# A state-space block and a feed-forward block in one kernel: token groups cut across batches

## The chip, the cores and the metric

The kernel runs on one core of a Trainium2 chip. The metric is the device time of one execution in microseconds, as the median of several runs. A core has a matrix engine (TensorE, in the profile PE, with its weight loads as PEld), a vector engine (VectorE, DVE), a scalar engine (ScalarE, ACT), a general engine (GpSimd, POOL) and a sync engine (SyncE, SP) that here only issues DMAs. Each engine works through its own list of instructions in order; between engines semaphores order the work. ACT and SP issue DMAs from their own lists, so an issue that has to wait holds up what stands behind it in that list.

## The reference

Two blocks follow each other. The first is a Mamba-2 scan with 4 batches, 8 heads, 768 tokens, head size 32, state size 16:

```python
chunk = 32
log_a = np.log(np.clip(a, 1e-06, 1.0))
for c in range(nc):
    cum = np.cumsum(la, axis=-1)
    L = np.exp(cum[:, :, :, None] - cum[:, :, None, :]) * causal
    M = np.einsum('bhin,bhjn->bhij', Cc, Bc) * L
    y_intra = np.einsum('bhij,bhjd->bhid', M, xc)
    y_inter = np.einsum('bhin,bhnd->bhid', Cc, state) * np.exp(cum)[..., None]
    y[:, :, sl] = y_intra + y_inter
    Bx = np.einsum('bhjn,bhjd->bhjnd', Bc, xc) * np.exp(cum[:, :, -1:] - cum)[..., None, None]
    state = np.exp(np.sum(la, axis=-1))[..., None, None] * state + np.sum(Bx, axis=2)
```

Its output, laid out as 3072 tokens (batch times sequence) by 256, goes through a feed-forward block with float64 weights of 256 x 2048 and 2048 x 256:

```python
h = x @ w_in
g = h * (1.0 / (1.0 + np.exp(-1.702 * h)))
return (g @ w_out).astype(np.float32)
```

All inputs but the weights are float32, and so is the output. The result does not depend on the chunk length; the kernel takes chunks of 64 tokens.

## The kernel before

**Tiling.** Tokens are worked in NG = 6 groups of TG = 512. A group has two pairs (PG = 2), a pair has two 128-token chunks, a 128-token chunk has two sides of 64 tokens, `SIDES`. Pair p stands for 128-token chunks 2p and 2p + 1 of the tokens counted through the batches: batch b and chunk c come from `divmod(2 * p, NC)` with NC = 6. So group 0 is the first 512 tokens of batch 0, group 1 its last 256 and the first 256 of batch 1, and so on. States run through the 64-token steps of one batch one after the other.

**The scan of one pair.** Decay matrices L come, for group 0, from cumulated logarithms (`cum`, by ACT's Ln and a DVE scan, then the matmuls of `differ`, line 554, and ACT's Exp, `decay_exp`, line 575); for pair 2 from a fan-out on PE and scans (`fan_all`); for later pairs from one DVE scan over the spread of a (`decay`, line 402). The spread is a DMA that copies a row of a scratch tensor to 64 partitions (`spread`, line 256). `ends` and `ends_first` make B times the decay to the chunk's end (Be), `score` the products C B^T (cb, line 680), `weigh` multiplies L by them (line 691), `gain` forms what a chunk adds to the state (A, line 711). `keep_first` (group 0) and `keep_both` (later groups) add gains up to states S; in group 0 by a DVE scan over all eight steps, with `drops` and `parts_first` preparing its operands. `finish` sums `intra` (line 828) and `inter` (line 816: C from the start of the chunk, CsT, times the state before) and ACT copies the sum to yT.

**Rows of decay since a chunk's start.** `since` is what `inter` and the states need. `spread_rows` loads a whole batch's row of a to all partitions (line 265), `clip_rows` and `decay_rows` turn it into `since[b]`; for batch 0 it comes from matmuls (`since_first`, and `fan_since` with `since_fanned`, lines 501 and 530).

**B and C.** For groups 0 and 2 to 5 they are loaded as blocks (zB, zC; `load_first` line 134, `load_blocks` line 124) and turned by DVE transposes (`turn_first` line 615, `turn_blocks` line 635); `turn_back` makes B by tokens again on PE for group 0.

**The feed-forward weights.** They arrive as float64 in ten pieces (`fetch`, line 180) and are narrowed to float32 on DVE and ACT: `fields` (lines 192, 195), `clamp` (ACT, lines 203, 204), `rounded` (line 208) and `join` (lines 222, 228). `fetch(1, held=True)` starts with a DVE memset of the tile, which is what lets its DMA go. `spread` has the same argument.

**The feed-forward block.** Groups 0 and the start of 1 are plain matmuls (`hidden` line 884, `project_all` line 982). From then on 2 x 2 block products are made with 7 multiplications: `first` (lines 940, 950; the copies by ACT are line 945, the SiLU line 917, the sums by DVE line 1072) and `product` (lines 1045, 1052), with operands mixed on DVE (`mix_in`, `mix_y`, `mix_g`, `mix_w`). In `first`, one PSUM bank X takes step "1", is copied by ACT, then takes step "6" on top, is copied, then "7" and "4": each of these matmuls waits for the copy before it. `turn_out` transposes a finished group on DVE and stores it by four DMAs per half (line 1103).

**What sets the order.** The order of each engine is written by hand: lists `in_hidden`, `in_project` and `after` hang work on places of group 0 and 1, and strings such as "4.1 4.5 4.2 P P 4.6 P L P 4.7 P P P 4.D" are run step by step (L is `more_loads`, which begins with the spread of pair 6). At the end `in_order` binds each engine to that order.

**Queues.** The build hands eight DMA semaphores out in turn to the DMAs of SP and ACT.

## Time and profile before

| what | us |
|---|---|
| median of 3 runs (350.42 to 353.03) | 351.38 |
| span of the profiled execution | 348.2 |
| PE busy in it | 341.8 |
| DVE, ACT, POOL busy | 254.8, 151.4, 14.0 |
| PE busy in 0 to 5, 5 to 10, 10 to 15, 15 to 20, 20 to 25 us | 3.79, 3.94, 4.76, 4.67, 4.43 |
| PE busy in 30 to 70 us | 40.0 |
| DVE busy in 50 to 60, 60 to 70, 70 to 80, 80 to 90 us | 9.35, 9.07, 9.86, 8.43 |
| first matmul of the hidden layer starts (line 884) | 17.47 |
| the second run of them, after the second weight piece, starts | 21.74 |
| DMA: packets, MB, share of 16 engines | 89980, 25.92, 34.1% (SP's and ACT's large queue) |

A line of a timeline gives the start in us from the beginning of the span, the length in us, the engine (a q behind it: its sequencer, which issues DMAs), the line of the kernel, the operation, what is written and read, the shape, and how often; in brackets stand the idle time of the engine before it and what ended that. The chain of waits is followed back from the last instruction, at each step to what released it. Times of one execution are compared with its own span; 3.2 us of the median lie outside it.

### The profile page before, as it was taken

The numbers are of one execution on the slowest core, as the hardware profiler recorded it, in microseconds if no ns is written. First come the engines' busy times: TensorE is split into PE (matmuls) and PEld (weight loads), VectorE is DVE, ScalarE is ACT, GpSimd is POOL, SyncE is SP. The second block draws the span as 40 slices with busy tenths as digits, with TensorE's granted clock in tenths as the row PEclk, the third lists the DMA queues.
The fourth block names the chain that finished last, engine by engine and source line by source line (L and its number), as shares of the span: only waits on it lengthen the run. The fifth ranks groups of instructions, "written<-read, shape, count | busy, mean of one in ns | idle before, by whom it ended". The sixth has DMA issues, their size and how long they took to land.

```text
span 348.2 us, 8126 instructions
## 1 busy us (share of the span) xinstructions
PE 341.8 (98%) x3386; PEld 273.1 (78%) x3386; DVE 254.8 (73%) x476; ACT 151.4 (43%) x348; POOL 14.0 (4%) x42
## 2 busy tenths in 40 slices
PE   7899999999999999999999999999999999999996
PEld 6634444557888888888888888888888888899996
DVE  5999999998679998839996548788454654455463
ACT  5598583107354323744342544432554321554320
POOL 8400000100000100000000000000000000000000
PEclk9999999999999999999999999999999999999999
DMA  6599997444527100445703027300000300000301
GB/s 158 118 347 200 260 219 172 78 85 80 107 53 133 44 0 10 69 93 102 111 22 55 2 75 121 65 0 3 0 4 2 61 2 0 0 2 0 62 0 61
DMA packets 89980, 25.92 MB, mean 74 GB/s; under 512 B 73432, under 2 KB 87128, under 8 KB 89944
## 3 DMA queue, kind: packets, MB, share of 16 engines
q1 hardware_dynamic: 89112, 24.88, 34.1%
q10 hardware_dynamic: 832, 0.52, 0.5%
q8 instruction: 26, 0.43, 0.5%
q14 instruction: 10, 0.08, 0.1%
HBM read 22.15 MB, written 3.24 MB: 73 GB/s over the span
## 4 chain that ended last, share of the span: by engine, by line
PE 93%; DMA 3%; DVE 3%; issue 1%; SPq 0%; DVEq 0%
PE acc L1045 28%; PE X L940 19%; PE Y L950 14%; PE h L884 9%; PE o L982 8%; PE acc L1052 7%; PE y L828 2%; PE cb L680 2%; PE y L816 1%; DMA bits<-in_moe_w_in_dram 1%; PE A L711 1%; DMA zB<-in_B_dram 1%; DMA az<-in_a_dram 1%; DVE p L192 1%; DVE m L208 0%
## 5 line engine op out<-in xcount | busy, mean ns | idle before, releaser
L945 ACT ACTIVATE ac<-X 128x256 f32<-128x256 f32 x76 | 29.0, 382 | 78.6 <-PE X L940 78.2
L1045 PE MATMUL acc<-mg,mw 128*128 128x256 f32 x192 | 54.5, 379 | 0.0
L917 ACT ACTIVATE gT<-gT 128x512 f32<-128x512 f32 (+1 forms) x76 | 39.3, 520 | 34.2 <-DVE gT L1072 33.5
L1072 DVE TENSOR_TENSOR gT<-Y,ac 128x512 f32<-128x512 f32 x38 | 26.2, 688 | 36.5 <-PE Y L950 29.9
L940 PE MATMUL X<-my,mi 128*128 128x256 f32 x152 | 45.2, 380 | 0.0
L1072 DVE TENSOR_TENSOR gT<-Y,b 128x256 f32<-128x256 f32 x38 | 15.8, 419 | 34.5 <-PE Y L950 34.5
L1045 PEld LDWEIGHTS acc<-mg,mw 128*128 128x128 f32 x192 | 36.5, 190 | 5.0
L884 PE MATMUL h<-yT,w_in 128*128 128x512 f32 (+2 forms) x108 | 35.7, 486 | 0.6 <-DVE w_in L228 0.6
L1045 PE MATMUL acc<-gT,w_out 128*128 128x256 f32 x128 | 35.5, 379 | 0.0
L884 PEld LDWEIGHTS h<-yT,w_in 128*128 128x128 f32 x108 | 18.3, 190 | 16.4 <-issue 13.2
L940 PEld LDWEIGHTS X<-my,mi 128*128 128x128 f32 x152 | 28.0, 190 | 4.1 <-ACT ac L945 0.4
L982 PE MATMUL o<-gT,w_out 128*128 128x512 f32 x64 | 28.6, 597 | 0.0
L908 DVE TENSOR_TENSOR mg<-gT 128x512 f32<-128x512 f32 x40 | 27.2, 681 | 0.0
L1045 PEld LDWEIGHTS acc<-gT,w_out 128*128 128x128 f32 x128 | 24.2, 190 | 3.4 <-ACT yT L855 0.2
L945 ACT ACTIVATE b<-X 128x256 f32<-128x256 f32 x38 | 14.6, 383 | 20.0 <-PE X L940 19.6
L940 PE MATMUL X<-yT,w_in 128*128 128x256 f32 x76 | 23.2, 389 | 0.0
L950 PE MATMUL Y<-yT,w_in 128*128 128x256 f32 x76 | 22.7, 381 | 0.0
L950 PE MATMUL Y<-my,mi 128*128 128x256 f32 x76 | 22.6, 379 | 0.0
L940 PE MATMUL X<-my,w_in 128*128 128x256 f32 x76 | 22.6, 381 | 0.0
L950 PE MATMUL Y<-yT,mi 128*128 128x256 f32 x76 | 22.5, 379 | 0.0
L982 PEld LDWEIGHTS o<-gT,w_out 128*128 128x128 f32 x64 | 11.8, 190 | 13.2 <-issue 12.4
L402 DVE TENSOR_TENSOR_SCAN L<-a,idents 128x1024 f32<-128x1024 f32 x9 | 20.5, 2278 | 0.4 <-DMA a<-scratch 0.4
(154 smaller groups left out, 544.5 us busy)
## 6 DMA issues: line engine op xcount, KB each, us to landing
a<-scratch SPq DMA_DIRECT2D x18, 256.0 KB, 5.2
bits<-in_moe_w_out_dram SPq DMA_DIRECT2D x8, 512.0 KB, 5.7
x<-in_x_dram SPq DMA_DIRECT2D x24, 128.0 KB, 3.3
out_dram<-ob SPq DMA_DIRECT2D x40, 64.0 KB, 1.9
bits<-in_moe_w_in_dram SPq DMA_DIRECT2D x8, 256.0 KB, 4.5
bits<-in_moe_w_in_dram SPq DMA_DIRECT2D x4, 512.0 KB, 9.2
b<-in_B_dram SPq DMA_DIRECT2D x20, 64.0 KB, 3.0
af<-in_a_dram SPq DMA_DIRECT2D x3, 384.0 KB
```

The source lines that it names most:

```text
L402: nc.vector.tensor_tensor_scan(out=L, data0=ra[p].rearrange("p k e -> p (k e)"), data1=idents.rearrange("p h i -> p (h i)"), initial=0.0, ...
L680: nc.tensor.matmul(out=s["cb"][side, r, k].rearrange("p (q i) -> p q i", q=Q), lhsT=BT[rows, k, side], rhs=CT[rows, k, :, side], start=Tru ...
L884: nc.tensor.matmul(out=h[:, cols], lhsT=w_in[:, f, k], rhs=yT[g][:, k, cols], start=(k == 0 and e == 0), stop=(k == NK - 1), skip_group_ch ...
L908: nc.vector.tensor_tensor(out=t[:, 0:2], in0=B[:, :, 1], in1=B[:, 0], op=ALU.subtract)
L917: nc.scalar.activation(o, i, AF.Silu, scale=GELU_SCALE)
L940: nc.tensor.matmul(out=s["X"], lhsT=lhsT, rhs=rhs, start=i == "1", stop=i == "4", skip_group_check=True)
L945: nc.scalar.activation(copy, s["X"], AF.Copy)
L950: nc.tensor.matmul(out=o, lhsT=lhsT, rhs=rhs, start=s.pop("new", False), stop=i != "5", skip_group_check=True)
L982: nc.tensor.matmul(out=o[c], lhsT=w_out[:, c, f], rhs=gT[g, f // 2][:, f % 2], start=(f == 0), stop=(f == NF - 1), skip_group_check=True)
L1045: nc.tensor.matmul(out=acc[g][0][i][:, cols], lhsT=w, rhs=h[:, cols], start=(j == 0 and k == 0 and (i, 0) in begins), stop=(j == NF // 2 - ...
L1052: nc.tensor.matmul(out=o[k] if type(o) is list else o[:, cols], lhsT=h[:, cols], rhs=w, start=(j == 0 and (i, k) in begins), stop=(j == NF ...
L1072: nc.vector.tensor_tensor(out=o, in0=v, in1=w, op=ALU.add)
```

## The change

A group is now one 128-token chunk of each of the four batches: pair p stands for chunk p // 2 of batches 0 and 1 (p even) or 2 and 3 (p odd), by `place`. So all four batches' states go forward together, two steps per group. Group 0's decays are cumulated over 128 columns for all 32 rows (batch and head) and not over 256 for 16; `differ` issues twice as many matmuls of half the width. The state of group 0 comes from ACT's copies of the gains and one multiply and add (`keep_first`, `carry_first`) in the place of the scan over eight steps. The second half of group 0's gains is formed after `finish`. Later states are made by `keep`: a product with the decay, then one DVE instruction per head of a quarter that takes the gains from PSUM. Rows of a are loaded per group, four DMAs for each; block loads of C and B take both of a group's pairs at once, eight DMAs each; a half group's store is 16 DMAs. The first loads have a new order and new queues, and x of pair 0 is issued by ACT between its Ln and its Exp table load. `fetch(1)` and the following ones come before `score`, `fields(0)` and `rounded(0)` later. `dense` gives way to `unread`, which puts three wide matmuls with unused results around the first `intra`.

```diff
-    def load_first(name, queues):
+    def place(p):
+        c, n = divmod(p, PG)
+        return c, 2 * n
+
+    def load_blocks(g, name, queues):
         src = {"B": B, "C": C}[name]
...
+            for q in range(Q):
+                queues[(Q * r + q) % len(queues)].dma_start(
+                    out=t[32 * r:32 * r + 32, q],
+                    in_=src[:, Q * r + q, g * P:(g + 1) * P].rearrange("b (i f) n -> i b (f n)", i=32))
...
-    def spread_rows(b):
-        raf[b] = raw.tile([P, NC, P], FP32, tag="af", name=f"af{b}", bufs=1)
-        nc.sync.dma_start(out=raf[b].rearrange("p c s -> p (c s)"),
-                          in_=a[b].unsqueeze(1).to_broadcast([NH, N, S]))
+    def spread_rows(g):
+        raf[g] = raw.tile([P, NB, P], FP32, tag="af", name=f"af{g}", bufs=2)
+        for b in range(NB):
+            nc.sync.dma_start(out=raf[g][:, b], in_=a[b, :, g * P:(g + 1) * P].unsqueeze(1).to_broadcast(
+                [NH, N, P]))
...
-    for r in range(R):
-        (nc.sync, nc.scalar)[r % 2].dma_start(
-            out=az0[32 * r:32 * r + 32].rearrange("p k s -> p (k s)"),
-            in_=a[:2, :, :TG].rearrange("b h (c s) -> (b h) c s", c=PG))
+    nc.sync.dma_start(out=az0, in_=a.rearrange("b h s -> (b h) s")[:, :P].unsqueeze(0).to_broadcast(
+        [R, NB * NH, P]))
...
-    load_first("C", [nc.scalar] * R)
-    load_first("B", [nc.sync] * R)
+    load_blocks(0, "C", [nc.scalar, nc.sync])
+    load_blocks(0, "B", [nc.scalar, nc.sync, nc.sync, nc.scalar, nc.sync, nc.sync, nc.scalar, nc.sync])
     fetch(0)
-    load(0, "x")
     load(1, "x")
...
     nc.scalar.activation(cum, az0, AF.Ln)
+    load(0, "x", nc.scalar)
     table(AF.Exp)
...
+    def keep_first(i):
+        if i == 0:
+            state[0] = ssd.tile([P, 2, NB, Q * D], FP32, tag="S", name="S0")
+        a, new = by_head(increment.pop((0, i))), by_head(state[0][:, i])
+        for q in range(Q):
+            nc.scalar.activation(new[:, :, q], a[:, :, q], AF.Copy, scale=part[:, q:q + 1])
+
+    def decayed(g, i):
+        t = ssd.tile([P, NB, Q * D], FP32, tag="old", name=f"old{g}_{i}", bufs=1)
+        e = i * H + H - 1
+        nc.vector.tensor_tensor(out=t, in0=state[g][:, 0] if i else state[g - 1][:, 1],
+                                in1=since[g][:, :, e:e + 1].to_broadcast([P, NB, Q * D]),
+                                op=ALU.mult)
+        return t
+
+    def carry_first():
+        plus(state[0][:, 1], state[0][:, 1], decayed(0, 1))
...
         for r in range(R):
             cols = slice(i * P + 32 * r, i * P + 32 * r + 32)
-            nc.sync.dma_start(out=rows[:, :, cols],
-                              in_=t[32 * r:32 * r + 32].rearrange("p (b e) -> p b e", e=32))
+            for b in range(NB):
+                nc.sync.dma_start(
+                    out=rows[:, b, :, cols],
+                    in_=t[32 * r:32 * r + 32, b * P:(b + 1) * P].rearrange("p (u e) -> p u e", e=32))
...
-    fields(0)
     ends_first(0)
     ends_first(1)
-    rounded(0)
-    score(range(PG), since_first)
-    weigh(0)
     fetch(1, held=True)
     for i in range(2, 6):
         fetch(i)
     rows_a(az, (nc.sync,))
+    score(range(PG))
+    since_first()
+    fields(0)
+    weigh(0)
     weigh(1)
-    drops()
-    gain(range(PG))
-    parts_first()
     for p in range(PG):
         since_start(p, nc.gpsimd)
+    gain(range(PG), (0,))
+    keep_first(0)
     clamp(0)
-    keep_first()
-    dense(2)
     finish(range(PG))
-    dense(0)
+    gain(range(PG), (1,))
+    keep_first(1)
+    rounded(0)
     join(0)
     fields(1)
     clamp(1)
+    carry_first()
```

## The prediction

> **What bounds the kernel now.** I read the page first, then the chain of waits in order of time, then the timelines of each engine over the first 22 us and over 76 to 113 us.

> ```profile
> span 348.2 us, 8126 instructions
> PE 341.8 (98%) x3386; PEld 273.1 (78%) x3386; DVE 254.8 (73%) x476; ACT 151.4 (43%) x348; POOL 14.0 (4%) x42
> PEclk9999999999999999999999999999999999999999
> PE 93%; DMA 3%; DVE 3%; issue 1%; SPq 0%; DVEq 0%
> ```

> TensorE (PE) is busy all through. In the chain it is the last to end from 21.74 us, where the second weight piece has been converted, until the closing stores. So a change can move the time in three ways: when PE begins its unbroken stretch, how much PE work lies in it, and whether a wait reaches PE inside it. First the start, ScalarE's timeline (start, length, engine and line, what, idle time before it):

> ```profile
> 3.75 0.44 ACTq L134 DMA_DIRECT2D zC<-in_C_dram  x1
> 4.81 0.42 ACT L343 ACTIVATE cum<-az 128x256 f32<-128x256 f32 x1 [1.17 <-DVE az L341]
> 5.25 1.28 ACT L285 ACT_TABLE_LOAD   x1
> 7.43 1.02 ACT L575 ACTIVATE L<-ab 128x1024 f32<-128x1024 f32 x1 [0.68 <-PE ab L554]
> 8.66 1.21 ACT L575 ACTIVATE L<-ab 128x256 f32<-128x256 f32 x4 [0.20 <-PE ab L554]
> ```

> Here the exponentials wait for PE, 0.68 and 0.20 us. Then a later place, SyncE's DMA queue (SPq), VectorE (DVE) and ACT:

> ```profile
> 78.25 1.00 SPq L150 DMA_DIRECT2D x<-in_x_dram  x2
> 88.01 0.67 SPq L265 DMA_DIRECT2D af<-in_a_dram  x1
> 91.40 5.40 SPq L1103 DMA_DIRECT2D out_dram<-ob  x8
> 101.87 1.27 SPq L256 DMA_DIRECT2D a<-scratch  x2
> ...
> 107.68 2.29 DVE L402 TENSOR_TENSOR_SCAN L<-a,idents 128x1024 f32<-128x1024 f32 x1 [0.42 <-DMA a<-scratch]
> 110.42 0.42 DVE L1072 TENSOR_TENSOR gT<-Y,b 128x256 f32<-128x256 f32 x1
> ...
> 110.87 0.42 ACT L917 ACTIVATE gT<-gT 128x256 f32<-128x256 f32 x1 [2.13 <-DVE gT L1072]
> 111.19 0.37 ACT L945 ACTIVATE ac<-X 128x256 f32<-128x256 f32 x1
> ...
> 112.03 0.59 PE L940 MATMUL X<-my,mi 128*128 128x256 f32 x2
> ```

> This is one chain. SP issues the spread of a for pair 6 at 101.87; its landing is the one DMA that any L402 scan waits for (0.42). Behind that scan in DVE's order stands the sum at 110.42; ACT sits 2.13 us for it; behind that on ACT stands the copy at 111.19, which ends at 111.56; the matmul at 112.03 adds to the same bank and may not start before. PE's slack there is 112.03 - 111.56 = 0.47 us. SP itself was idle from 88.68 to 91.40 and from 96.80 to 101.87, 2.72 + 5.07 = 7.8 us.

> **The start, step by step.** The build hands out eight DMA semaphores in turn over SP and ACT together: a DMA may be issued once the eighth before it has landed. That is in the order of the built programs, and the rows show it (the last zC is issued at 3.75 although ACT's issue before ended at 3.70). Rows: an issue takes 0.42 to 0.44 us (the first on each queue 0.6 to 0.8), landing is 2.0 to 2.7 us after issue; I take 2.3. Before, 12 loads come ahead of the weights (4 az, 4 C, 4 B); after, 17 (1, 8, 8).

> SP after: az at 0.80, C at 1.6, 2.25, 2.7, 3.2, B at 3.7, 4.5, 5.0, 5.5, 6.0 (from the second B on held by the C eight before). ACT: C at 0.95, 1.5, 2.0, then 3.8 (waits for the C of 1.6), B at 4.3, 4.8, 5.25. ACT's Ln stands behind that last issue, so it starts at 5.7 and not 4.81, although az, now one DMA, lands earlier. Behind Ln stand pair 0's two x issues, each waiting for a B load that SP issued: 5.0 + 2.3 = 7.3 and 5.5 + 2.3 = 7.8. Behind them stands the Exp table load: 7.8 + 0.55 + 1.28 + 0.2 = 9.9 us for the first exponential, 2.5 us later than 7.43. PE no longer limits it (its masks' sums end near 9.6: half the scan width saves some 0.3 of 0.69 us, twice the small L554 matmuls cost some 0.2 per pair by the 0.86 us that 64 records of A take). The five exponentials then run back to back and end at 9.9 + 1.02 + 1.21 = 12.1, against 9.87.

> Part of it is given back. Be started 0.6 us late (10.48) because DVE was at `fields(0)`, whose first step took 1.72 us beside POOL's L648 and 0.43 us elsewhere. After: Be to 12.8, fields 0.85, weigh 2.35, so weigh ends at 16.0 against 14.09. Removed behind it: the scan over states 1.22 and its two copies 0.70 on DVE, the POOL copy 0.99. Added there: a multiply and an add of 128x256 (`carry_first`, 2 x 0.42), which wait for ACT's copies of the second half's gains. Of the 28 inter matmuls 16 remain, 0.95 of 1.67 us; 16 of the 32 gains now stand between them and h, 0.4. So h begins near 18.6 (17.47 before). The second piece: first piece ready at 16.0 + 3 x 0.69 = 18.1, fields 0.85, then `carry_first` waiting for yT's four copies (to 19.0) and two more (0.75): ends 20.2; then 0.68 + 0.85 + 0.69 + 0.69 = 23.1 against 21.60. With landings of 2.0 us it is 22.5. I take +1.2 us. Ends: -0.9 if the waits on ACT bind nowhere (fetch(1) is then let go 2.6 us earlier, since its memset moves ahead of the fields), +1.8 with landings of 2.7 us.

> [...]

> **PE's work in the unbroken stretch.** The fanned rows go (L501 and L530, 0.62 us in the chain at 36.33). Twelve inter matmuls move from group 0 into later groups: 28 cost 0.97 us in the chain, 32 cost 1.09, so three groups x 0.12 = 0.36. Gains: the same 144 in all. Sum -0.3 us.

> **What lies beside it.** On DVE from 57 to 92 us: row scans of 512 and not 768 (1.76 becomes about 1.2) but one more of them with its clip and its wait for POOL (2.1), states by 4 narrow products and 2 sums per group (2.0) for 1.72 and 3.2, and no `since_fanned` (0.85) and starts (0.17) earlier. Net +0.5 to +1 us; the cover is DVE's wait of 3.07 us at 95.03 and the 4 us between the states' end (88.48) and their matmuls (92.43). ACT loses its copies of gains (12 x 0.33). Stores in the tail keep their sizes.

> **The queue at pair 6.** Between x at 78.25, which waits for PE's last use of that buffer, and the spread, SP now issues 16 block loads and not 8, 4 row loads and not 1, 32 stores and not 8: 35 more. Stores: 24 more x 0.475 (the median 0.425 of a 32-partition block load plus 0.05 between issues) = 11.4. Blocks 8 x 0.47 = 3.8, rows 3 x 0.55 = 1.7. Sum 16.9. Less the 7.8 us that SP was idle, less 1.2 for one of the eight store issues of before, which took 1.68 (I do not carry it over), less 0.9 since no block loads follow the spread any more (5.05 us to land with them, 4.0 the least of 18): the scan starts 7.0 us later. Less PE's slack of 0.47: PE stands still 6.5 us, once, and PE's time is not made up. Ends: 3.0 with the cheapest rows (0.31 to 0.36 per issue), 8.5 with 0.53 per store. Later groups have room: there some 31 us lie between the stores' end and the next spread (172.3 to 203.8).

> Sum: 348.2 + 1.2 - 0.3 + 6.5 = 355.6 us of span; around the span lie 351.38 - 348.2 = 3.2 us of the median: 358.8. I say **358.5**.

> [...]

> **Rivals.** *The queue hides it (not slower).* One mechanism: SP's spare time. It decides where 35 issues fit into 7.8 us of idle, 2.1 us of saved waits and 0.47 of slack, 10.4 / 35 = 0.30 us each. The smallest issue in the trace is 0.31, the median 0.425, which speaks against it; against my sum speaks that the issue of a store is known only at 512 runs of 128 B, never at 128. Then the time is 351.4 + (-0.9 to +1.8) - 0.3 = 350.2 to 352.9. *Half hidden*: stall 1 to 3 us, 353 to 355.5. *The start gains more than my rows allow* (ACT's issues do not hold Ln and Exp, DVE's shorter work shows in full) and no stall: below 347.9; it would need 3.5 us, and the largest saving I can point to is 2.6. *The stall brings the clock or a second wait with it*: above 361.5.

> **How the numbers follow.** Forecast (354.9 to 361.5) 0.60, hidden 0.16, half hidden 0.08, large gain 0.09, above 361.5 0.07. The range 350 to 361.5 leaves out the large gain and the highest case. One per cent, 3.5 us, is what a measurement can tell from no change: below 347.9 is 0.09; above 354.9 is 0.60 + 0.07 + a fifth of half hidden = 0.68; the rest, 0.23, is within.

> **What would show it.** Right: ACT's Ln after 5 us with x issues between it and the table load, first exponential past 9 us; SP busy without a break from 79 to past 105 (on the clock of before), the spread issued last, a DVE scan that waits some 7 us for it, and one hole of several us in PE at an X matmul. Wrong: store issues below 0.3 us, or a scan that waits under 1 us; a first exponential at 7.5; PE idle at another place, or PE at a lower clock.

## The result and the profile after

The kernel after takes **373.66 us** (median of 4 runs, 372.25 to 374.68), the kernel before in the same comparison 350.95 us. The ratio is 1.064 with a 95% interval of 1.059 to 1.069: slower, and by three times what was forecast (358.5, at most 361.5). Some executions of a kernel take over 1.5% longer than its fastest; ratios and intervals leave them out, medians do not, and the profile of the run with x alone is one of them. The profiled execution has a span of 372.2 us. From its page, the span, TensorE's row, the clock in 40 slices of 9.3 us, and the shares of the chain that ended last:

```profile
span 372.2 us, 8393 instructions
PE 351.3 (94%) x3452; PEld 279.5 (75%) x3452; DVE 250.2 (67%) x458; ACT 148.5 (40%) x333; POOL 11.8 (3%) x38
PEclk9889999999899879999999999999999999999999
PE 88%; issue 3%; SPq 3%; DMA 2%; DVE 2%; ACT 1%; ACTq 0%; DVEq 0%
```

TensorE stands idle for 20.9 us, not 6.4, and is itself busy for 9.5 us more, though its work hardly changed: where the clock row shows 8 or 7 the same matmul takes longer (where the clock is 0.50, from 127.66 to 134.49 us, a pair of 128x256 matmuls takes 1.06 us, and 0.59 where it is 1.00). "issue" in the chain, time in which an engine waits for nothing that the profile shows, rose from 1% to 3%.

ScalarE's timeline (start, length, engine and line, what; in brackets the idle time before it and its releaser) answers to the five lines of before:

```profile
4.48 1.41 ACTq L127 DMA_DIRECT2D zB<-in_B_dram  x3
5.94 0.31 ACT L331 ACTIVATE cum<-az 128x128 f32<-128x128 f32 x1 [3.65 <-DMA zC<-in_C_dram]
6.81 1.15 ACTq L144 DMA_DIRECT2D x<-in_x_dram  x2
7.99 1.28 ACT L278 ACT_TABLE_LOAD   x1 [1.75 <-DMA zB<-in_B_dram]
9.40 2.10 ACT L527 ACTIVATE L<-ab 128x1024 f32<-128x1024 f32 x5
```

Ln starts at 5.94 (5.7 forecast), the exponentials at 9.40 (9.9) and end at 11.50 (12.1). `weigh` ends at 16.1 (16.0). Up to there the forecast of the start holds. Then the place of pair 6, from the timelines of SyncE's queue, VectorE, ScalarE and TensorE:

```profile
101.22 2.61 SPq L260 DMA_DIRECT2D af<-in_a_dram  x4
103.93 16.67 SPq L1021 DMA_DIRECT2D out_dram<-ob  x32
120.70 1.13 SPq L250 DMA_DIRECT2D a<-scratch  x2
...
125.78 2.29 DVE L385 TENSOR_TENSOR_SCAN L<-a,idents 128x1024 f32<-128x1024 f32 x1 [6.85 <-DMA a<-scratch]
...
128.96 0.42 ACT L834 ACTIVATE gT<-gT 128x256 f32<-128x256 f32 x1 [8.56 <-DVE gT L989]
...
129.71 1.22 PE L857 MATMUL X<-my,mi 128*128 128x256 f32 x2 [5.84 <-ACT ac L862]
130.72 1.06 PE L962 MATMUL acc<-gT,mw 128*128 128x256 f32 x2
```

This too came as forecast: 32 stores in 16.67 us (0.43 us is the median of one, two took 1.04 and 1.31), the spread behind them, a scan that waits 6.85 us (7.0), a hole of 5.84 us at an X matmul (6.5). What was not forecast is the last line: two matmuls that took 0.59 us before the hole take 1.06 behind it. And there are holes with no releaser at all: nothing that the profile shows ends the wait. The table of TensorE's waits (line, releaser: sum in us, times, longest), then its timeline at the first of them:

```profile
PE X L857 <- ACT ac L862: 5.8, 1, 5.8
PE A L649 <- issue: 3.5, 1, 3.5
PE y L744 <- issue: 2.6, 3, 1.4
PE cb L621 <- issue: 2.4, 2, 1.6
```

```profile
20.89 0.57 PE L649 MATMUL A<-x,Be 64*32 64x64 f32 x25
24.98 0.31 PE L649 MATMUL A<-x,Be 64*32 64x64 f32 x7 [3.52 <-issue]
25.23 2.07 PE L801 MATMUL h<-yT,w_in 128*128 128x512 f32 x2
```

Six waits, 8.5 us, where before had one of 0.55. At 21.46 TensorE stops in the middle of a row of 32 equal gains, 25 done and 7 to go. The windows of after give the granted clock (PEclk) and the busy share of the DMA engines in each stretch:

```profile
15.00:20.00 5.00, 5.00 (x164) 3.48 (x152) 4.24 (x7) 2.45 (x6) 1.34 (x3) 0.66 0.97 274
25.00:30.00 5.00, 5.00 (x14) 2.21 (x14) 3.95 (x9) 4.55 (x8) 0.00 (x0) 0.66 0.55 118
90.00:100.00 10.00, 8.38 (x156) 6.80 (x155) 9.65 (x18) 2.31 (x6) 0.20 (x1) 0.85 0.31 60
100.00:120.00 20.00, 20.00 (x271) 17.05 (x271) 10.16 (x24) 9.49 (x23) 0.00 (x0) 0.99 0.33 55
130.00:140.00 10.00, 10.00 (x37) 8.40 (x37) 7.90 (x15) 3.22 (x9) 0.84 (x3) 0.78 0.00 1
```

The third number from the right is the clock: 0.66, 0.66, 0.85 and 0.78 where a stretch of half clock lies in the window, 0.99 where hardly any does. Three of these stretches follow the holes of 3.52, 1.62 and 5.84 us. The first, from 15.0 to 18.4 us, lies ahead of the hole of 3.52, behind waits of 0.91 and 0.82 us at 9.8 and 12.2. Laying the same matmul of both traces side by side gives an account of the delay:

| stretch (us in after) | delay at its end | what it adds |
|---|---|---|
| to the first hidden matmul, 25.2 | 7.75 | 1.1 forecast; some 3.1 ahead of the hole, 2.1 of them from 13.5 to 17.5, mostly at half clock; the hole of 3.52 |
| to 44.9 | 7.90 | 1.69 half clock; the w_in wait (0.57) and the fanned rows gone |
| to 86 | 7.84 | nothing |
| to 99 | 11.56 | a hole of 1.62 and some 0.5 of shifts, 1.58 half clock |
| to 132 | 19.8 | 5.84 (pair 6), 2.45 half clock |
| to the end | 23.45 | holes of 1.39, 0.57 and 0.63 and what follows them |

### The profile page after: what moved, and what is told of

Read it like the earlier page. It is cut to its first block, busy times and chain, and to the rows that moved or that the text cites. A ratio compares the mean times of both kernels' runs of the same rounds, so it can differ in the third digit from the quotient of the medians.

```text
span 372.2 us, 8393 instructions
## 1 busy us (share of the span) xinstructions
PE 351.3 (94%) x3452; PEld 279.5 (75%) x3452; DVE 250.2 (67%) x458; ACT 148.5 (40%) x333; POOL 11.8 (3%) x38
## 4 chain that ended last, share of the span: by engine, by line
PE 88%; issue 3%; SPq 3%; DMA 2%; DVE 2%; ACT 1%; ACTq 0%; DVEq 0%
PE acc L962 25%; PE X L857 17%; PE Y L867 13%; PE h L801 10%; PE o L899 8%; PE acc L969 7%; PE y L744 2%; PE cb L621 2%; SPq L1021 2%; PE y L732 2%; PE A L649 2%; DMA a<-scratch 1%; PE y L428 1%; DMA zC<-in_C_dram 1%; DVE L L385 1%
## 5 line engine op out<-in xcount | busy, mean ns | idle before, releaser
L857 PE MATMUL X<-my,mi 128*128 128x256 f32 x152 | 46.2, 387 | 5.8 <-ACT ac L862 5.8
L801 PE MATMUL h<-yT,w_in 128*128 128x512 f32 (+2 forms) x108 | 38.8, 521 | 0.0
L857 PEld LDWEIGHTS X<-my,mi 128*128 128x128 f32 x152 | 28.5, 193 | 10.1 <-ACT ac L862 6.2
L801 PEld LDWEIGHTS h<-yT,w_in 128*128 128x128 f32 x108 | 20.2, 207 | 17.5 <-issue 15.2
L385 DVE TENSOR_TENSOR_SCAN L<-a,idents 128x1024 f32<-128x1024 f32 x9 | 20.5, 2276 | 6.9 <-DMA a<-scratch 6.9
L862 ACT ACTIVATE b<-X 128x256 f32<-128x256 f32 x38 | 14.6, 384 | 20.6 <-PE X L857 20.2
L867 PE MATMUL Y<-yT,w_in 128*128 128x256 f32 x76 | 22.7, 381 | 0.0
L899 PEld LDWEIGHTS o<-gT,w_out 128*128 128x128 f32 x64 | 11.8, 190 | 13.2 <-issue 12.2
```

The costliest lines, as they stand in the source:

```text
L385: nc.vector.tensor_tensor_scan(out=L, data0=ra[p].rearrange("p k e -> p (k e)"), data1=idents.rearrange("p h i -> p (h i)"), initial=0.0, ...
L801: nc.tensor.matmul(out=h[:, cols], lhsT=w_in[:, f, k], rhs=yT[g][:, k, cols], start=(k == 0 and e == 0), stop=(k == NK - 1), skip_group_ch ...
L857: nc.tensor.matmul(out=s["X"], lhsT=lhsT, rhs=rhs, start=i == "1", stop=i == "4", skip_group_check=True)
L862: nc.scalar.activation(copy, s["X"], AF.Copy)
L867: nc.tensor.matmul(out=o, lhsT=lhsT, rhs=rhs, start=s.pop("new", False), stop=i != "5", skip_group_check=True)
L899: nc.tensor.matmul(out=o[c], lhsT=w_out[:, c, f], rhs=gT[g, f // 2][:, f % 2], start=(f == 0), stop=(f == NF - 1), skip_group_check=True)
```

## The experiments

**What the holes have in common.** Counting all of TensorE's instructions in the trace from 0, in the order of their starts (matmuls, weight loads and the semaphore instructions between them), the waits without releaser in after stand before numbers 449, 961, 2241, 3777, 4801 and 5825. Each is 193 over a multiple of 256; the one of before stands at 705, which is 193 over as well. The page's table of DMA queues has a queue of instructions (reads, MB, share):

```profile
q8 instruction: 27, 0.44, 0.5%
```

That is 16 KB per read. The 6952 instructions of TensorE in after have 27 numbers of that kind, as many as there are reads; the 6823 of before have 26, and it has 26 reads. So my theory was: instructions come in blocks of 256, and where a burst of small matmuls eats a block up faster than the next one is fetched, TensorE stands still at the block's end. Rivals: the new groups' own work holds it there; or the fetch is late because the DMA engines are full of weights.

*Pair 6's rows first:*

```diff
-    at(after, "H1", lambda: turn_out(0, 0), lambda: turn_out(0, 1))
+    at(after, "H1", lambda: spread(p), lambda: turn_out(0, 0), lambda: turn_out(0, 1))
...
     def more_loads():
-        spread(p, held=True)
```

> The two row loads of pair 6 are issued at the place of before, ahead of group 0's 32 stores; nothing else is changed. Theory (SP's queue): the scan of pair 6 no longer waits 6.9 us for its rows, TensorE's hole of 5.8 us at 123.9 to 129.7 goes, and with it the slow clock behind it, in which another 2.45 us were lost: 373.7 - 5.8 - 2.45 = 365.4 us, PEclk full between 120 and 140 us. Rival 1 (another releaser is late there, the block loads of pairs 6 and 7 or the DMA queue itself): the hole stays at 4 us or more, 371.5 to 374. Rival 2 (the hole goes, but the slow clock after it does not come from the hole): 367.8.

Measured: 367.06 us, ratio 1.043 (1.0386 to 1.0474). The timelines of its SyncE queue and VectorE, and the window of its TensorE:

```profile
103.10 1.13 SPq L250 DMA_DIRECT2D a<-scratch  x2
104.33 16.98 SPq L1021 DMA_DIRECT2D out_dram<-ob  x32
...
118.04 2.28 DVE L385 TENSOR_TENSOR_SCAN L<-a,idents 128x1024 f32<-128x1024 f32 x1
```

```profile
120.00:130.00 10.00, 10.00 (x48) 8.81 (x47) 9.27 (x20) 4.36 (x11) 0.83 (x3) 1.00 0.57 99
```

The scan waits for nothing, the hole is gone, and the clock stays at 1.00. Between 99 and 132 us the delay now changes by -0.3 and not by +8.3: 8.5 us for hole and clock, 8.25 expected. Some 2 us come back at the block end of 164 us, 1.75 long here and followed by half clock, against 1.39 without it in after. So the theory holds, rival 1 falls with the hole, and rival 2, in which the clock is no consequence of the hole, falls.

*64 instructions more*, whose results nobody uses: `keep_busy(4, 16)` in place of `keep_busy(4, 0)`.

> 16 tiny matmuls that nobody reads (64 instructions on TensorE) are added in the first microseconds, when TensorE is idle; the data flow is as in the kernel after. TensorE's idle stretches without a releaser stand at instruction 449, 961, 2241 and 3777 of its stream, all 193 over a multiple of 256. Theory 1 (instructions come in blocks of 256, and a block is late where a burst of small matmuls eats it up faster than it is fetched): every such place moves 64 instructions ahead in the work. The hole in the second half of the gains at 21.5 goes, and one of 1.5 to 3.5 us appears in the reads of y before it, near 20.5; the holes at 94.5 (1.6 us) and 171.8 (1.4 us) shrink or move by 64 instructions: 370 to 374 us. Theory 2 (something in the work itself holds TensorE there, a wait that the trace does not show): the holes stay at the same matmuls and of the same length, 373.5 to 374 us.

Measured: 370.15 us, 1.0557 (1.0495 to 1.0619). TensorE's timeline:

```profile
18.25 0.79 PE L732 MATMUL y<-CsT,S 32*64 32x64 f32 x25
21.92 0.44 PE L732 MATMUL y<-CsT,S 32*64 32x64 f32 x7 [2.88 <-issue]
```

The gains run through without a hole; it now stands 64 instructions earlier in the work, in the reads of y, and again at number 961 of the stream. The holes of 1.62, 0.57 and 0.63 are gone and the one of 1.39 is 0.68. A wait of the work itself would have stayed with its matmul. Of the 6.1 us by which TensorE is ahead of after near 99 us, 3.1 are lost again: the hole at pair 6 grows to 8.93, since SyncE issues that spread only 3.2 us earlier (117.51).

*The control: 96 more in the kernel before* (`keep_busy(4, 24)`).

> The control, on the kernel before: 24 tiny matmuls that nobody reads (96 instructions on TensorE) in its idle first microseconds. In before the fourth place 193 over a multiple of 256 (number 961) lies among the long matmuls of the hidden layer, where 256 instructions last 20 us and more; with 96 more it lies at work instruction 865, 12 from the end of the reads of y at 17.0 us. Theory (a block of instructions is late where a burst of small matmuls eats it up): before too now gets a hole without a releaser near 17 us, 1.4 to 3.5 us long, and loses that and some slow clock: 352.5 to 355 us. Rival (the holes belong to something else that the change brings): 351 to 351.5 us, no hole above 0.8 us.

Measured: **358.30 us, ratio 1.0206 (1.0149 to 1.0262)**, nearly twice the largest loss expected. The kernel before, with 24 tiny matmuls in idle time that nobody reads, is 7.5 us slower. Its TensorE timeline, and its page's clock:

```profile
16.30 1.43 PE L816 MATMUL y<-CsT,S 32*64 32x64 f32 x46 [0.35 <-DVE S L740]
20.11 0.79 PE L816 MATMUL y<-CsT,S 32*64 32x64 f32 x10 [2.38 <-issue]
```

```profile
PEclk9969999999999999999999999999999999999999
```

A hole at number 961, half clock behind it (2.6 us), and two more of 1.38 and 1.41 us at numbers 4801 and 5825, in the bursts of y at 211 and 266 us. This settles that the holes do not belong to the change. Before is fast in part because its block ends happen to fall on long matmuls.

The traces also hold the reads themselves, with their times. In all 57 waits without releaser of 0.25 us and more, in all 17 traces, TensorE goes on 1.22 to 1.69 us after the end of the last of them, though the waits differ from 0.31 to 3.52 us. At 21.46 in after, the read starts 0.87 us into the hole, at 22.34, and ends at 23.38; TensorE goes on at 24.98. So these holes are waits for instructions; what fills the time from the end of a read to the next instruction is not shown.

*Weights later:* `fetch(2)` to `fetch(5)` and `rows_a` go behind `fields(1)`.

> The weight loads 2 to 5 and the rows of a are issued behind the first group of gates (some 8 us later) instead of at 12 to 19 us; nothing is left out. Theory 1a (the block of instructions that TensorE lacks at 21.5 is queued behind weight loads on the DMA engines): the hole of 3.5 us shrinks to the 1.4 to 1.6 us of the later holes of its kind, and the slow clock behind it (1.7 us) with it: 370 to 372 us, unless the weights themselves come too late for the hidden layer. Theory 1b (only the place of the block's end in the burst counts): the hole stays at 3 us or more, 373 to 374 us or later by what the weights lose.

Measured: 374.41 us, 1.0668 (1.0614 to 1.0722), the same as after. Its timeline and its window show why two effects cancel:

```profile
20.86 1.00 PE L649 MATMUL A<-x,Be 64*32 64x64 f32 x32
21.79 3.70 PE L801 MATMUL h<-yT,w_in 128*128 128x512 f32 x8
```

```profile
15.00:20.00 5.00, 5.00 (x164) 3.43 (x153) 4.34 (x9) 2.49 (x6) 1.33 (x3) 0.66 0.08 26
```

With the DMA engines at 0.08 and not 0.97 the read of this block starts at 19.24 and not 22.34; the 32 gains run in one piece, at the same block end, and the hidden layer starts 3.44 us earlier than in after. But weights that come late raise its delay from 4.3 to 7.1 us by 39 us, and by 82 us it is 8.3, more than in after (7.8). So the length of a hole has two parts: the place in a burst (0.6 to 2.0 us in later groups), and, in the first 25 us, the weight loads (3.52 us with the DMA engines at 0.97 in 15 to 20 us, no hole there with 0.08).

*ScalarE's queue.* Two runs: x(0) back on SyncE (alone), and B as well, on top of the run with 224 more below.

```diff
-    load_blocks(0, "B", [nc.scalar, nc.sync, nc.sync, nc.scalar, nc.sync, nc.sync, nc.scalar, nc.sync])
+    load_blocks(0, "B", [nc.sync])
     fetch(0)
+    load(0, "x")
...
-    load(0, "x", nc.scalar)
```

> The two loads of x(0) go back from ScalarE's queue to SP's, ahead of x(1). Theory (ScalarE is held by its own DMA issues): Exp's table is loaded 1.1 us earlier, the exponentials of L end near 10.3 instead of 11.5, and all that depends on them moves up by about 1 us. What the time gains depends on the hole of 3.5 us at 21.5, in which TensorE waits for no data: if it is set by where TensorE stands in its own stream, it moves up too, 372.5 us; if it is set by when the DMA engines are free, the gain is swallowed there: 373.5 to 374. Rival (ScalarE's two issues cost nothing, the blocks' landing sets the head): no group of the head moves by more than 0.3 us, 373.5 to 374.

> The run with 224 more (361.8), and all loads of B and x(0) issued by SP, so that ScalarE issues the four loads of C alone ahead of its Ln. Theory (ScalarE's own DMA issues hold the head): Ln starts by 4.9 us and not near 6, TensorE's first masks' sums about 1 us earlier, the first matmul of the hidden layer at 19.8 and not 20.8; 360.8 us. Rival (what SP issues later lands later, and the head hangs on that): Ln earlier, but the first hidden matmul where it was or later, 361.8 to 363.

Measured: x alone 375.29 us, 1.0602 (1.051 to 1.0695; its two shorter executions 369.77 and 374.96), no difference from after that can be told. Exp's table was loaded at 6.63 and not 7.99, but the exponentials ended at 11.42 against 11.50: the second pair's then waited 0.42 us for TensorE's sums. With B too, 363.79 us, 1.0353 (1.0325 to 1.0380), 2 us worse than without. Ln started at 4.98 and not 6.10, but VectorE's timeline has

```profile
11.57 1.08 DVE L568 STREAM_TRANSPOSE Bt<-zB 128x512 f32<-128x512 f32 x1 [3.51 <-DMA zB<-in_B_dram]
```

2.4 us later than with B on two queues (9.13). The second run's rival is right: what one queue saves in ScalarE's time it loses in B's landing. In these traces x on ScalarE costs next to nothing.

*Both edits, and the block ends shifted further.* Pair 6's rows first together with 16 tiny matmuls, then with 56 (224 instructions), then with 16 and weight loads 4 and 5 and `rows_a` later.

> Both edits that helped, together: pair 6's row loads ahead of group 0's stores, and 64 more instructions on TensorE at the start. If the two causes are separate, the gains add: 373.7 - 8.5 (hole and slow clock at 124) - 3.5 (the holes at 94.5 and later and their slow clock, gone with 64 more) - 1.5 (the start) = 360, within 1.5. If the holes at block ends come back elsewhere once the hole at 124 is gone, as it was with the first edit alone (2 us given back at 164): 362 to 364.

> As the run before, with 224 more instructions and not 64: the block ends lie 224 instructions earlier, which is 32 later for the block behind. The one that in the kernel after falls on the gains at 21.5 now falls on the hidden layer's long matmuls. If only the place of the block end counts, the hole there goes and the time falls 2 to 4 us below that of the run with 64 more: 356 to 358. If the weight loads hold the block up until 24 us wherever it is needed, the hole is still there, 1 us shorter at most: 359 to 361.

> As the run with 64 more, and weight loads 4 and 5 and the rows of a go behind the first group of gates; 2 and 3 stay. With weight loads 2 to 5 moved, the hole of 3.5 us was gone but weights came late for the hidden layer (holes of 1.9 us at 30.7 and 1.2 at 39.2). If the transfers on the DMA engines hold the instruction block up, half of them does half: a hole of 0 to 1.5 us in place of 2.9 near 19, no late weights: 357 to 358.5. If not: as the run with 64 more, 360.

Measured: 362.72 (1.032, 1.0265 to 1.0374), 361.76 (1.0306, 1.0252 to 1.0359) and 358.39 us (1.0194, 1.0139 to 1.0248). The first is where its second case had it, 2.7 us above the plain sum: a block end at 160 us costs 1.2 again, and a wait for VectorE shows. The second lies above both of its ranges (356 to 358, 359 to 361). With 224 more there is no hole at a block end between 15 and 25 us, and the hidden layer starts at 20.8; but the added matmuls, the pads, themselves delay the masks' sums by 0.9, and holes of 1.1 to 1.5 us appear at 158, 213 and 267. The shift moves holes, it does not abolish them. Half of the weights later is worth 4.3 us on top of the first, where 1.5 to 3 were expected, and the hole at number 961, 2.33 us in the first, is gone; its time is in the range expected.

The wait for VectorE, from the waits of the run with 224 more:

```profile
PE A L649 <- DVE Be L449: 1.5, 1, 1.5
```

It is a real cost of the change: the scan over group 2's rows of a stands ahead of the second pair's scan of L. *Rows' scan later* (`decay_rows(2)` behind `mix_y(1)`):

> The run with 224 more (361.8), and group 2's scan over the rows of a (with its 0.53 us of waiting for POOL) on VectorE behind the scan of the second pair's L and the sums of Y, not ahead of them. Theory (that extra scan makes TensorE wait for Be): TensorE's wait of 1.5 us at 87.6 to 89.1 goes, no other comes in its place: 360.3 us. Rival (the states, which need that scan, are then late): a wait of 1 us or more at the state matmuls near 96, 361.5 to 362.5.

Measured: 361.97 us, 1.0312 (1.0279 to 1.0345), unchanged by its time. In its trace the wait is gone and the delay does not rise near 90 us (by 1.9 before), but 0.9 comes back as a wait for VectorE at 131, and in this execution TensorE had half clock from 12.71 to 22.95 us, 3.5 us more in the start. The time does not show a gain; the wait's cause is shown.

*28 fewer* (no `unread`, `keep_busy(0, 0)`), with pair 6's rows first, and *all*: these two, B and x on SyncE and the rows' scan later:

> Pair 6's rows first, and 28 instructions fewer on TensorE instead of 224 more (256 - 28 = 228, so block ends lie almost where they lay there): the four idle matmuls at the start and the three wide ones around the first reads of y are left out, whose results nobody uses. If the place of the block's end counts, no matter how it came there: no hole at 21.5, first hidden matmul at 19.0 to 20.3 (20.8 there; the pads' 0.9 us and up to 1 us of the wide matmuls saved), 360 to 361.3 us. If the wide matmuls were needed for the clock: PEclk below 0.9 between 15 and 25 us, and 362 or more.

> All edits of the three runs before it together: 28 fewer, pair 6's rows first, B and x(0) on SP, the rows' scan later. If they add: 358 to 359.5 us. What then is left above the kernel before (351) would be the head (about 1 us) and the holes at block ends in later groups (1.3 to 2 us each with 224 more, at 158, 212 and 267). If the time falls below 351, the change itself is worth something once these are gone, which I do not expect.

Measured: 365.20 (1.041, 1.0378 to 1.0443) and 363.32 us (1.0359, 1.0308 to 1.0411), the first as its second case had it (362 or more), the second worse than expected. The holes at 13 and 21.5 do not come. But in the first, TensorE works at half clock from 7 to 28 us by the lengths of its matmuls (`ab` takes 1.28 us per 64 and not 0.91, one of the hidden layer at 25.3 us 1.06 and not 0.59), and the hidden layer starts at 23.4. Its windows show a clock of 1.00 there all the same: the trace has no record of the clock ahead of 28.5 us, and where there is none the windows count it as full. All six executions lie above the four with 224 more, so the unread matmuls seem to earn their place. In the run with all edits the clock is half from 17.1 to 27.3 us, and B and x land late (waits of 2.3 and 2.0 us).

**What the rest is.** Three runs on top of rows' scan later: 24 tiny matmuls once more inside group 0's hidden layer, so that the later groups' block ends move on (first), two wide unread matmuls ahead of `turn_back`'s transposes, meant to fill the wait there (second), both (third).

```diff
         h = bank(f"h{g}_{f}")
+        if (g, f) == (0, 12):
+            pads(24, h)
...
-        o = bank("b").rearrange("p (j r k e) -> p j r k e", j=PG, r=R, k=2)
+        o = bank("b")
+        unread(o[:, :4 * H], 2, True)
+        o = o.rearrange("p (j r k e) -> p j r k e", j=PG, r=R, k=2)
```

> The run with 224 more and the rows' scan later (362.0), and 24 tiny matmuls (96 instructions) once more in the middle of group 0's hidden layer, so that for the groups behind it the block ends lie 320, that is 64 modulo 256, earlier in the work, as in the runs with 64 more, which had no holes at 212 and 267. Theory (the rest of the loss in the groups is the place of the block ends): the holes of 1.5, 1.9 and 1.5 us at 160.8, 215.6 and 270.3 go, 0.5 us for the added matmuls: 357 to 358.5. Rival (those holes belong to the new groups' own work): they stay, 362 to 363.

> The run with 224 more and the rows' scan later (362.0), and two wide matmuls that nobody reads in TensorE's wait of 1.4 to 1.8 us ahead of the transposes of B's ends (two tiny ones fewer at the start, so that block ends stay). Theory (this wait, coming after an idle start, is what lets the clock fall in some executions; half clock from 12 to 24 us cost 3.5 us there): PEclk 1.00 from 5 to 25 us, first hidden matmul at 20.5 to 21.5 in place of 24.3, 359 to 360.5, and the runs closer together. Rival (the clock falls for another reason): PEclk still below 0.8 somewhere between 10 and 25 us, 361.5 to 363.

> The two edits of the runs before it together. If each takes away what its theory says: 355 to 356.5 us, and what is left above the kernel before is the head (about 2.5 us) and waits below 1 us. If it comes out at 351 or below, the new groups as such are no slower than the old; if it stays above 358, a cost that I have not named is left.

Measured: **356.62 (1.0165, 1.0145 to 1.0185)**, 361.22 (1.0297, 1.0278 to 1.0315) and 356.73 us (1.0172, 1.0148 to 1.0196). From the page and TensorE's waits of the first:

```profile
PEclk9999999999999999999999999999999999999999
```

```profile
PE y L744 <- issue: 2.0, 2, 1.3
PE b L580 <- ACT L L527: 1.4, 1, 1.4
PE busy L414 <- DVE ones L291: 1.2, 1, 1.2
PE h L803 <- DVE p L186: 1.1, 1, 1.1
```

With 96 more instructions without use the kernel is 5.4 us faster, and the holes at 216 and 270 are gone, as this run's theory had it; 1.26 at 157 and 0.73 at 19.6 are left. Not all of the 5.4 is theirs. Between the two profiled executions (5.9 us apart) these holes make up 3.4; the other one also had the half clock in its start, 2.5 us at the first hidden matmul, and a wait for VectorE at 131, 1.4 with what follows it, and the added matmuls take some 0.6 back. The two executions with rows' scan later at a mean clock of 1.00 took 360.19 and 360.56 us: at equal clock the gain is some 3.8.

The second edit did not fill the wait. TensorE's timeline:

```profile
11.95 1.13 PE L428 MATMUL b<-ones 128*128 128x256 f32 x4 [1.60 <-ACT L L527]
```

The unread matmuls wait for ScalarE as the transposes did: 1.60 us, against 1.76 with rows' scan later and 1.42 in the first run. The clock was at 1.00 through the start and the first hidden matmul stood at 21.00, as this run's theory had them, but the first run had that clock too without them. On record is the mean clock of each execution: 0.995 or more in nine of the 14 with this start and no filler (224 more, rows' scan later, the first run) and in all 11 with it. So an effect of the unread matmuls is possible but not shown, and it is not that of a filled wait. The time stays at 361, between the two ranges expected, with the holes of the later groups (1.2 to 1.8 us) in it. The third run lies 0.2 us above the range expected. Whether the wait is what lets the clock fall, these runs leave open; the steps of 3.41 us in the last section speak for it. No version beat the kernel before. In the trace of the best one the first hidden matmul is 4.4 us late, at 158 us the delay is 6.25, at the end 6.4.

## Why the prediction was wrong

- *The start, +1.2 us, h near 18.6:* **this step failed**, 7.75 us at the first hidden matmul. Its terms for data held (Ln, exponentials, `weigh` within 0.6 us). What failed is the stretch behind them: I added matmuls by their durations, as if a burst were always supplied and always at full clock. It met half clock from 15.0 to 18.4 us, behind waits of under 1 us each, and a hole of 3.5 us at a block end. The change puts more small matmuls into the start (`differ` issues twice as many), and with that moves every block end behind it.
- *The hold on ScalarE:* right for Ln, which waits behind the issues of B. The part laid to x(0)'s issues was wrong: without them the exponentials ended 0.1 us earlier.
- *PE's work, -0.3 us:* the fanned rows' part is seen in the account (between 30.5 and 44.9 us the delay falls by 0.8). But the step says nothing of holes inside the stretch, which cost some 3.6 us near 95 us (with half clock) and as much again behind 132.
- *Beside it, cover of 3.07 us on VectorE:* too wide. The second pair's scan came 1.5 us late for the gains once other delays were gone.
- *The queue at pair 6, +6.5 us:* right in mechanism, place and nearly in size (5.84); 0.475 us from one store to the next is what most of the 32 took. "PE stands still 6.5 us, once" left out the 2.45 us of half clock behind it. The sum has no term for a lower clock: in before the granted clock is 1.00 from 4.2 us to the end, and behind the first matmul TensorE waits 0.57 us at most. The forecast itself had an idle stretch of 6.5 us, and the run shows half clock from 127.66 to 134.49 us behind its hole of 5.84.
- *The rival that ended above 361.5* ("the stall brings the clock or a second wait") was given 0.07. It is what came, together with the instruction blocks that no rival had.

Of the 22.7 us, the edits account for 17: 6.6 with pair 6's rows first, 5.3 with 224 more, 5.4 with 96 more inside (the rows' scan -0.2 between). That is an account in this order; the parts are not independent, as the runs with one edit alone show, and some 1.6 of the last go with the clock. Some 6 us stay with the change and the pads: a later start above all.

## What to carry to other kernels

Before judging an edit that adds or removes many small TensorE instructions, shift the kernel before by some tens of unused ones: a few per cent can hang on the places 193 modulo 256 (2.1 in before with 96 more), and such an edit is then judged with its luck. An idle stretch on TensorE is to be priced with the half clock that can follow it: here 1.58, 1.69 and 2.45 us behind holes of 1.62, 3.52 and 5.84. A queue that issues in order should issue what an engine waits for ahead of the stores that nobody waits for (6.6 us here).

## What the hardware showed

| run, step (us) | idle inside it | TensorE busy | clock behind it |
|---|---|---|---|
| after, 93.53 to 96.94 | the hole of 1.62 | 0.52 | half |
| rows' scan later, 9.30 to 12.71 | the wait of 1.76 | 0.48 | half |
| rows' scan later and 24 inside, 10.81 to 14.22 | the wait of 1.42 | 0.58 | full |
| rows first and 64 more, 17.36 to 20.78 | half of the hole of 2.33 | 0.65 | full |
| rows first and 64 more, 20.78 to 24.19 | the other half | 0.66 | full |

- The cost behind the holes of 3.52 and 5.84 us fits these steps: 1.69 us is half of one, and 2.45 is half of the 4.8 us that were left of two when TensorE went on at 129.7.
- SyncE took 0.43 us (median) to issue a DMA of 16 KB for a store in a row of 32, as for a block load; two of the 32 took 1.04 and 1.31 us.
